# Row picks of the first two slots as two wide comparisons, with reordered first tiles, join, routing and shared slot

## The chip, the cores and the metric

One core of a Trainium2 chip runs the whole program. The metric is the device time of one execution in microseconds (us). The engines named below are PE (matrix products), DVE (vector), ACT (activation functions), POOL (GpSimd) and SP, which only issues transfers; ACT and POOL issue some transfers too.

## The reference

Three layers run one after the other: banded attention, a layer of 8 experts with 4 soft slots each, and a layer of 8 experts of which each token takes its best two.

```python
# attention: B=2, H=8, S=768, D=64; 8 global keys, 96 local ones
scores = scale * q @ k.T - slopes * dist            # masked to is_global | is_local
a = exp(scores - max); a /= a.sum + 1e-9; x = a @ v # x: [1536, 512]
# soft layer, 32 slots
logits = x @ phi
d = softmax(logits over tokens); c = softmax(logits over slots)
slot_out[e] = relu((d.T @ x)[e] @ w1[e]) @ w2[e]
x = c @ slot_out
# top-2 layer
noisy = x @ w_gate + log1p(exp(x @ w_noise)) * noise
top2 = the two largest of noisy; top2_w = softmax of the two
out[token] += top2_w * (relu(x[token] @ w1[e]) @ w2[e])   # for both experts
```

## The kernel before

Attention works on 12 tiles of 128 tokens (`NT`). The loop of `attention_near` (tile number `T`) issues by hand, for all engines: `load_k`, `load_q` and `load_v` on SP, mixed with `more_w`, which loads the first layer's weights piece by piece as `PACE` allows; `scores(T)` on PE; `maxima` (DVE) and `exps` (ACT); `inverse` (DVE, L221 and L222) and `norm` (POOL, L234); the transposes of tile T-1 (`turn`, L244, copied out at L249 or L251); the products with the values of tile T-2 (`values`, L270). A k load brings three tiles (816 KB, `KLOADS`), a v load two (512 KB, `VLOADS`); v tiles live in two buffers, so the load of tiles 4 and 5 waits until tile 2 has read tiles 0 and 1. `fill` (L398) and `warm` (L566, L799) issue matmuls whose results nobody reads; `NWARM` (L136) does so before the first tile. The bias of the scores is made from the table `dist` (L162, L165) at L392 and L402.

After the last tile `seg` and the lines from L566 join the running sums of the soft layer: a chain of small steps between PE, DVE and ACT (the join). Then `ffn_a` (L720) and `ffn_b` (L766) compute the 8 soft experts on PE in fp32; each fp32 matmul shows as two instructions, and four of them lie side by side in the array. `ffn_b` sums all experts into one PSUM tile `op` of 512 columns, which ACT (L793) and DVE (L794) copy out by halves; L803 turns the result into `soT`.

Then comes the routing, by hand on PE, DVE, ACT and POOL: noisy logits (L998 to L1013), best two (L1029, L1032), counts and positions of each token within its expert (L1035 to L1105), which give each token a `key` if it is among the rows of the first two slots (128 rows each, both of expert 0). `placed` compares the key of each of the 12 token groups with the 256 row numbers (`places`), one DVE instruction per group (L1252), into `z`; `direct` multiplies `z` with the slot weights of the tokens on PE (L1236), and L1276 copies the product out as the input of slots 0 and 1. `rows6` is a table of the row numbers, each repeated 6 times; `onehot` (L1116) uses it for the general slots. All constant tables come from `k16`, loaded at L808; ACT expands them (`table`, L1019).

From there 24 slots of 128 rows run one after the other (L1219, L1220, L1228, L1327), each with 24 products of 512 columns on PE. Beside them `rank_steps` prepares the weights of the next expert (`w_hi` on ACT L894, `w_lo` on DVE L897, `BASE` gives the place), and `Shared` (slot 24, shared by four experts, L1146 to L1202) runs within slots 18 to 21.

Of the kernel before, what the change touches and what calls it, by code (L numbers as in the profile page):

```python
# [22 lines left out]
NWARM = 16  # L23
# [5 lines left out]
KLOADS = {1: 3, 4: 6, 6: 9}  # L29
VLOADS = {0: 2, 4: 4, 6: 6, 8: 8, 10: 10}  # L30
FILL = {0: 3, 1: 4}
KP = 95
# [32 lines left out]
def emit(tc, d, near=True, stop=None):  # L65
    nc = tc.nc
    es = ExitStack()
    with es:
# [87 lines left out]
        if near:  # L156
# [5 lines left out]
            nc.sync.dma_start(out=dist[1], in_=d["dist"][1])  # L162
            load_q(1, nc.scalar)
            load_k(1)
            nc.sync.dma_start(out=dist[0], in_=d["dist"][0])  # L165
# [53 lines left out]
        def inverse(st):  # L219
            r = sm.tile([128, 4], F32, name="r", bufs=3)  # L220
            nc.vector.tensor_scalar(r, st, 1e-9, None, ALU.add)  # L221
            nc.vector.reciprocal(r, r)  # L222
            return r
# [162 lines left out]
        def attention_near():  # L386
# [24 lines left out]
            for T in range(NT + 1):  # L411
                new, b0, b1 = T < NT, 2 * T, 2 * T + 1
                more_w(PACE(b0))
                if T in KLOADS:
                    load_k(KLOADS[T], 3)
                if T + 3 < NT:
                    load_q(T + 3)
# [30 lines left out]
                for o in outs:  # L448
                    o()
                if new:  # L450
# [32 lines left out]
            fill(2, ps_t.tile([128, 512], F32, name="pt"))  # L483
            psl = logits(*SEGS[NT - 1])
            next(old)
            s_hand.close()
# [197 lines left out]
        nc.sync.dma_start(out=more, in_=d["more"])  # L684
        soT = cs2.tile([128, 4, 32], F32, name="soT")
# [52 lines left out]
        op = ps_y.tile([128, 512], F32, name="y")  # L738
# [22 lines left out]
        def ffn_b(e):  # L761
            hT = hTs.pop(e)
            for i in range(2):
                for g in range(4):
                    f = 4 * i + g
                    nc.tensor.matmul(op[32 * g:32 * g + 32, :], hT[:, f % 2, f // 2, :], units[4 * e + 2 + i][:, g],  # L766
                                     start=(e == 0 and i == 0), stop=(e == NE - 1 and i == 1), tile_position=(0, 32 * g))
# [25 lines left out]
        nc.scalar.activation(os_[:, 0:256], op[:, 0:256], AF.Copy)  # L793
        nc.vector.tensor_copy(os_[:, 256:512], op[:, 256:512])  # L794
# [13 lines left out]
        nc.sync.dma_start(out=k16, in_=d["c16"])  # L808
# [188 lines left out]

        nc.scalar.activation(ex, pl[:, :, 8:16], AF.Exp)  # L998
# [8 lines left out]
        nc.vector.scalar_tensor_tensor(t1, u_, -1.0, ex, ALU.add, ALU.subtract)  # L1007
        nc.vector.reciprocal(rc, u_)
        ttt(t1, t1, rc, ALU.mult)
        ttt(t1, t1, noise, ALU.mult)  # L1010
# [6 lines left out]
        def table(t, a):  # L1017
            n, m = t.shape[1], t.shape[2]
            nc.scalar.activation(t, k16[:, a:a + n].unsqueeze(2).to_broadcast([128, n, m]), AF.Copy)  # L1019

        table(exp24, K24)
# [11 lines left out]
        table(slot6, KSLOT)  # L1033
# [39 lines left out]
        table(rows6, 361)  # L1073
# [5 lines left out]
        K1.g_mm((2, 3))  # L1079
# [24 lines left out]
        keys = scratch([128, NT], F32)  # L1104
        ttt(keys, key16[:, 0:NT], key16[:, NT:], ALU.min)  # L1105
# [127 lines left out]
        def direct(z):  # L1233
            pct = pm_([128, 256])
            for t in range(NT):
                nc.tensor.matmul(pct, crow[:, t, 0:128], z[:, t], start=(t == 0), stop=(t == NT - 1))  # L1236
            return pct

        places = k16[:, 361:617]
# [8 lines left out]
        z = scratch([128, NT, 256], F16)  # L1248

        def placed(a, b):  # L1250
            for t in range(a, b):
                nc.vector.tensor_scalar(z[:, t], places, keys[:, t:t + 1], None, ALU.is_equal)  # L1252
# [10 lines left out]
        K1.g_scale_a()  # L1263
        placed(0, 2)
        K0.w_scale_a()
        K0.w_pow_a()
        placed(2, 4)
        K0.w_pow_b(lambda: placed(4, 5), lambda: placed(5, 6))
        placed(6, NT)
# [28 lines left out]
        def slot_y(j, hh):  # L1298
# [34 lines left out]
            if j < NOWN - 1:  # L1333
                ys = (z.rearrange("p t c -> p (t c)")[:, 1024 * j:1024 * j + 1024].bitcast(F32) if j < 2 else wk3.tile([128, 512], F32, name="ys", bufs=2) if j % 3 else
# [93 lines left out]
        def rank_steps(r):  # L1428
# [30 lines left out]
            k(6, "w_lo", 1)  # L1459
# [4 lines left out]
            k(9, "w_lo", 2)  # L1464
# [339 lines left out]
```

## Time and profile before

| what | us |
|---|---|
| median of 3 runs | 312.25 |
| lowest and highest of them | 311.44, 312.27 |
| the profiled execution | 313.0 |
| its span, first to last instruction | 310.9 |
| busy: PE, ACT, DVE, POOL | 294.2, 201.9, 199.4, 131.7 |

The profiled execution took 313.0 us, of which 310.9 are its span and 2.1 lie around it. It is 0.75 us above the median of the runs. A busy PE counts matmuls whose results nobody reads as well, so 95% says little by itself: a stage is read by what PE waited for in it, and by the transfers that landed just before. In the timeline, each line has the start, the time from start to end of a group of equal instructions, the engine, the source line, output and input; in brackets stands how long the engine sat idle before it and what released it. A letter q behind an engine's name stands for its queue, which issues transfers.

### The profile page before, as it was taken

The numbers are of one execution on the slowest core, as the hardware profiler recorded it, in microseconds if no ns is written. First come the engines' busy times: TensorE is split into PE (matmuls) and PEld (weight loads), VectorE is DVE, ScalarE is ACT, GpSimd is POOL, SyncE is SP. The second block draws the span as 40 slices with busy tenths as digits, with TensorE's granted clock in tenths as the row PEclk, the third lists the DMA queues.
The fourth block names the chain that finished last, engine by engine and source line by source line (L and its number), as shares of the span: only waits on it lengthen the run. The fifth ranks groups of instructions, "written<-read, shape, count | busy, mean of one in ns | idle before, by whom it ended". The sixth has DMA issues, their size and how long they took to land. (4 is left out here: it accounts for less than half of the span.)

```text
span 310.9 us, 7834 instructions
## 1 busy us (share of the span) xinstructions
PE 294.2 (95%) x2889; PEld 171.5 (55%) x2889; DVE 199.4 (64%) x728; ACT 201.9 (65%) x479; POOL 131.7 (42%) x169
## 2 busy tenths in 40 slices
PE   8579999999999999998999999999999999999990
PEld 3368887887765443444544445544454445544570
DVE  2868779878553000499786878879586595995110
ACT  3888977977313110499789786859688686795320
POOL 3856644754210010232726828563517335432252
PEclk9999999999998999999999999999999999999997
DMA  7999999989999999999799998498999943423444
GB/s 244 347 396 403 399 396 401 406 312 348 383 411 368 399 407 404 411 408 354 292 345 413 373 327 161 68 363 268 246 335 333 348 71 51 52 29 39 59 57 54
DMA packets 30715, 89.26 MB, mean 287 GB/s; under 512 B 2752, under 2 KB 6848, under 8 KB 30672
## 3 DMA queue, kind: packets, MB, share of 16 engines
q1 hardware_dynamic: 25840, 80.70, 67.9%
q0 software_dynamic: 4544, 7.48, 16.0%
q8 instruction: 25, 0.41, 0.5%
q10 hardware_dynamic: 288, 0.52, 0.5%
q14 instruction: 18, 0.15, 0.1%
HBM read 78.55 MB, written 10.14 MB: 285 GB/s over the span
## 5 line engine op out<-in xcount | busy, mean ns | idle before, releaser
L1327 PE MATMUL y<-w2hl,hh 128*128 128x512 f16 x528 | 119.8, 379 | 0.0
L1327 PEld LDWEIGHTS <-hh 128*128 128x128 f16 x528 | 49.8, 98 | 57.7 <-issue 3.3
L216 ACT ACTIVATE Tt<-Tt,nm 128x167 f32<-128x167 f32 x96 | 40.5, 425 | 5.2 <-DVE nm L210 5.2
L1228 DVE SCALAR_TENSOR_TENSOR hh<-h,hh 128x512 f16<-128x512 f32 x46 | 29.5, 683 | 20.6 <-ACT hh L1220 20.6
L234 POOL TENSOR_TENSOR Pb<-Tt,r 128x668 f32<-128x668 f32 x24 | 31.2, 1300 | 26.4 <-ACT Tt L216 19.2
L897 DVE SCALAR_TENSOR_TENSOR w2hl<-w,pm,w2hl 128x1024 f16<-128x1024 f32 x28 | 35.2, 1280 | 1.4 <-issue 0.7
L1345 POOL DMA_INDIRECT out_y<-ys,sidx x14 | 23.0, 1642 | 25.2 <-ACT ys L1339 17.1
L1364 POOL DMA_INDIRECT cT<-ctab,gidx x25 | 28.4, 1137 | 11.5 <-issue 5.5
L1220 ACT ACTIVATE hh<-h 128x512 f16<-128x512 f32 x46 | 25.1, 598 | 11.9 <-PE h L1219 11.9
L894 ACT ACTIVATE w2hl<-w,pm 128x1024 f16<-128x1024 f32 x28 | 31.2, 1147 | 0.2 <-DVE pm L850 0.2
L865 ACT ACTIVATE w2hl<-w 128x1024 f16<-128x1024 f32 x28 | 29.6, 1059 | 0.0
L210 DVE CUSTOM_DVE_ANT_0 Tt<-s,bias 128x167 f32<-128x167 f32 x96 | 25.7, 324 | 3.0 <-PE s L200 2.0
L1345 POOL DMA_INDIRECT out_y<-c,sidx x7 | 11.9, 1704 | 35.3 <-ACT w2hl L894 12.3
L244 PE MATMUL pt<-c,Pb 128*128 128x128 f32 x176 | 24.1, 278 | 2.6 <-ACT PT L251 1.6
L251 ACT ACTIVATE PT<-pt 128x512 f32<-128x512 f32 (+1 forms) x36 | 18.8, 556 | 9.6 <-PE pt L244 9.3
L244 PEld LDWEIGHTS pt<-c,Pb 128*128 128x128 f32 x176 | 18.8, 141 | 6.8 <-issue 3.1
L270 PE MATMUL px<-PT,vt 128*64 128x128 f32 x352 | 21.9, 276 | 0.0
L270 PEld LDWEIGHTS px<-PT,vt 128*64 128x64 f32 x352 | 19.0, 137 | 2.5 <-issue 2.0
L200 PE MATMUL s<-kx,qd 64*64 64x167 f32 x384 | 17.0, 307 | 2.6 <-DVE nm L210 1.7
L216 ACT ACTIVATION_READ_ACCUMULATOR Tt<-Tt,nm 128x1 f32 x96 | 18.2, 189 | 0.0
L756 POOL MEMSET hT<- 128x256 f32 x8 | 2.3, 311 | 35.5 <-PE y L766 23.5
L1219 PEld LDWEIGHTS <-Gst 128*128 128x128 f16 x192 | 12.7, 98 | 6.2 <-issue 0.8
(323 smaller groups left out, 482.4 us busy)
## 6 DMA issues: line engine op xcount, KB each, us to landing
w<-in_w2b SPq DMA_DIRECT2D x14, 1024.0 KB, 11.7
w<-in_w1a SPq DMA_DIRECT2D x24, 512.0 KB, 9.9
w<-in_w2a SPq DMA_DIRECT2D x12, 1024.0 KB, 10.8
x<-in_w1b SPq DMA_DIRECT2D x12, 1024.0 KB, 12.6
w<-in_w2a SPq DMA_DIRECT2D x8, 512.0 KB, 8.5
w<-in_w1a SPq DMA_DIRECT2D x4, 1024.0 KB, 10.7
vt<-in_va SPq DMA_DIRECT2D x6, 512.0 KB, 8.9
out_y<-w2hl SPq DMA_DIRECT2D x1, 3072.0 KB, 11.3
```

The lines of the kernel that those rows point to most:

```text
L210: nc.vector.tensor_tensor_reduce(S[i][:, k], bank(p, t), bias[:, int(i // 2 % 6 == 0), p, t], -0.125, 1e30, ALU.add, ALU.min, nm[:, k:k + 1])
L216: nc.scalar.activation(Tt[:, k], Tt[:, k], AF.Exp, bias=nm[:, k:k + 1], scale=-1.0, accum_out=st[:, k:k + 1])
L234: nc.gpsimd.tensor_tensor(wide(Pn, 33, 264 + 64, 528, 167), Pu.rearrange("p (a t) c -> p a t c", t=2), rb(167), ALU.mult)
L244: nc.tensor.transpose(pt[:, ch, t], Pn[:, 2 * (n % 2) + t, 136 * ch:136 * ch + 128], ident)
L270: nc.tensor.matmul(px[64 * h:64 * h + 64, p, :], vv[:, c:c + 64], cols_, start=(ch == 0 or m == 0), stop=(ch == 1))
L865: nc.scalar.activation(w2hl[:, self.r, 1, 2 * q:2 * q + 2], self.quarter(q), AF.Abs, accum_out=self.wm[:, q:q + 1])
L894: nc.scalar.activation(w2hl[:, self.r, 0, 2 * q:2 * q + 2], self.quarter(q), AF.Copy, scale=self.sw)
L897: nc.vector.scalar_tensor_tensor(w2hl[:, self.r, 1, 2 * q:2 * q + 2], self.quarter(q), self.sw, w2hl[:, self.r, 0, 2 * q:2 * q + 2], ALU.m ...
L1228: nc.vector.scalar_tensor_tensor(hh[:, 1, 4 * q:4 * q + 4], phs[q], 0.0, hh[:, 0, 4 * q:4 * q + 4], ALU.max, ALU.subtract)
L1327: nc.tensor.matmul(py, hh[:, hx, f], w2hl[:, e, wx, f], start=(n == 0), stop=(n == 23))
L1345: o = nc.gpsimd.indirect_dma_start(out=out, out_offset=bass.IndirectOffsetOnAxis(ap=sidx[:, j:j + 1], axis=0), in_=ys, in_offset=None, com ...
L1364: nc.gpsimd.indirect_dma_start(out=cgf[:, place(n)], out_offset=None, in_=ctab, in_offset=bass.IndirectOffsetOnAxis(ap=gidx[:, n:n + 1], a ...
```

## The change

The change has nine parts.

1. Start: `NWARM` goes from 16 to 9; both `dist` loads move from the SP queue to the ACT queue, in front of the second q load; the k load of tiles 3 to 5 moves from T = 1 to T = 0; each k load of the loop goes ahead of the weights of its turn; five `fill` matmuls are added in T = 1 behind the transposes.
2. `inverse`: the add of 1e-9 becomes a `scalar_tensor_tensor` with the same tile as both inputs.
3. Join: two more `fill` matmuls at the end of `attention_near`.
4. `op` becomes two tiles of 256 columns; `ffn_b` computes the first half of all columns, then the second.
5. `k16` is loaded ahead of the second layer's weights, and its three tables are expanded before the routing's first exponential, not between its steps.
6. The product with `noise` (L1010) moves from DVE to POOL and ahead of the reciprocal.
7. `placed` becomes two comparisons of 128 x 1536 elements, against `rows6`; `keys` becomes f16 with a second row, keys - 2, for the second slot; the rows of `z` are read by PE with a step of 6 elements; `direct` gets ten warming matmuls of 256 columns between its own.
8. `K1.g_mm((2, 3))` moves behind `K0.w_pow_a`, `K1.g_scale_a` behind that.
9. For the last expert `w_lo` of quarters 1 and 2 each move one place later.

```diff
-NWARM = 16
+NWARM = 9
-KLOADS = {1: 3, 4: 6, 6: 9}
+KLOADS = {0: 3, 4: 6, 6: 9}
+MORE = {1: 5}
...
             nc.sync.dma_start(out=negs, in_=d["negs"])
-            nc.sync.dma_start(out=dist[1], in_=d["dist"][1])
+            nc.scalar.dma_start(out=dist[1], in_=d["dist"][1])
+            nc.scalar.dma_start(out=dist[0], in_=d["dist"][0])
             load_q(1, nc.scalar)
             load_k(1)
-            nc.sync.dma_start(out=dist[0], in_=d["dist"][0])
...
-            nc.vector.tensor_scalar(r, st, 1e-9, None, ALU.add)
+            nc.vector.scalar_tensor_tensor(r, st, 1e-9, st, ALU.add, ALU.max)
...
-                more_w(PACE(b0))
                 if T in KLOADS:
                     load_k(KLOADS[T], 3)
+                more_w(PACE(b0))
...
                 for o in outs:
                     o()
+                fill(MORE.get(T, 0))
...
-            fill(2, ps_t.tile([128, 512], F32, name="pt"))
+            ft = ps_t.tile([128, 512], F32, name="pt")
+            fill(2, ft)
             psl = logits(*SEGS[NT - 1])
             next(old)
+            fill(2, ft)
...
         nc.sync.dma_start(out=more, in_=d["more"])
+        nc.sync.dma_start(out=k16, in_=d["c16"])
...
-        op = ps_y.tile([128, 512], F32, name="y")
+        op = [ps_y.tile([128, 512], F32, name="y")[:, 0:256] for _ in range(2)]
...
-            for i in range(2):
-                for g in range(4):
-                    f = 4 * i + g
-                    nc.tensor.matmul(op[32 * g:32 * g + 32, :], hT[:, f % 2, f // 2, :], units[4 * e + 2 + i][:, g],
-                                     start=(e == 0 and i == 0), stop=(e == NE - 1 and i == 1), tile_position=(0, 32 * g))
+            for c in range(2):
+                for i in range(2):
+                    for g in range(4):
+                        f = 4 * i + g
+                        nc.tensor.matmul(op[c][32 * g:32 * g + 32], hT[:, f % 2, f // 2, :],
+                                         units[4 * e + 2 + i][:, g, 256 * c:256 * c + 256], start=(e == 0 and i == 0),
+                                         stop=(e == NE - 1 and i == 1), tile_position=(0, 32 * g))
...
+        for t, a in ((exp24, K24), (slot6, KSLOT), (rows6, 361)):
+            n, m = t.shape[1], t.shape[2]
+            nc.scalar.activation(t, k16[:, a:a + n].unsqueeze(2).to_broadcast([128, n, m]), AF.Copy)
         nc.scalar.activation(ex, pl[:, :, 8:16], AF.Exp)
...
+        nc.gpsimd.tensor_tensor(t1, t1, noise, ALU.mult)
         nc.vector.reciprocal(rc, u_)
         ttt(t1, t1, rc, ALU.mult)
-        ttt(t1, t1, noise, ALU.mult)
...
-        keys = scratch([128, NT], F32)
-        ttt(keys, key16[:, 0:NT], key16[:, NT:], ALU.min)
+        keys = scratch([128, 2, NT], F16)
+        ttt(keys[:, 0], key16[:, 0:NT], key16[:, NT:], ALU.min)
+        nc.vector.tensor_scalar(keys[:, 1], keys[:, 0], -2.0, None, ALU.add)
...
-                nc.tensor.matmul(pct, crow[:, t, 0:128], z[:, t], start=(t == 0), stop=(t == NT - 1))
+                nc.tensor.matmul(pct, crow[:, t, 0:128], z[:, t // 6, :, :, t % 6], start=(t == 0), stop=(t == NT - 1))
+                if 0 < t < NT - 1:
+                    nc.tensor.matmul(wy[:, 0:256], warmw[:, 0:128], warmw[:, 0:256], start=True, stop=True)
...
-        z = scratch([128, NT, 256], F16)
-        def placed(a, b):
-            for t in range(a, b):
-                nc.vector.tensor_scalar(z[:, t], places, keys[:, t:t + 1], None, ALU.is_equal)
+        zf = scratch([128, 3072], F16)
+        z = zf.rearrange("p (q h r i) -> p q h r i", q=2, h=2, i=6)
+        def placed(q):
+            ttt(z[:, q], keys[:, :, 6 * q:6 * q + 6].unsqueeze(2).to_broadcast([128, 2, 128, 6]),
+                rows6.unsqueeze(1).to_broadcast([128, 2, 128, 6]), ALU.is_equal)
...
-        K1.g_scale_a()
-        placed(0, 2)
         K0.w_scale_a()
         K0.w_pow_a()
-        placed(2, 4)
-        K0.w_pow_b(lambda: placed(4, 5), lambda: placed(5, 6))
-        placed(6, NT)
+        K1.g_mm((2, 3))
+        K1.g_scale_a()
+        placed(0)
+        K0.w_pow_b()
+        placed(1)
...
-            k(6, "w_lo", 1)
+            k(6 if r < NE - 1 else 9, "w_lo", 1)
...
-            k(9, "w_lo", 2)
+            k(9 if r < NE - 1 else 10, "w_lo", 2)
```

## Rows read from the trace of the kernel before

**Rows 1.** Busy time by stretch: us, each engine's busy us (instructions), PE's granted clock, DMA share, GB/s.
```profile
20.00:40.00 20.00, 19.01 (x294) 16.31 (x296) 14.77 (x73) 16.99 (x64) 11.55 (x17) 1.00 1.03 402
...
280.00:300.00 20.00, 20.00 (x163) 10.01 (x162) 6.94 (x23) 8.58 (x12) 5.11 (x6) 1.00 0.36 48
```

**Rows 2.** Timeline of the first tiles.
```profile
1.18 4.97 PE L136 MATMUL psl<-xT 128*128 128x512 f16 x16 [1.18 <-DVE xT L133]
...
6.08 1.36 PE L200 MATMUL s<-kx,qd 64*64 64x167 f32 x32
...
6.17 0.51 DVE L392 TENSOR_TENSOR bias<-xs,negs 128x334 f32<-128x334 f32 x1 [4.63 <-DMA xs<-in_dist]
...
7.57 3.17 POOL L392 TENSOR_TENSOR bias<-xs,negs 128x668 f32<-128x668 f32 x2 [4.42 <-DMA xs<-in_dist]
...
8.05 1.53 DVE L392 TENSOR_TENSOR bias<-xs,negs 128x668 f32<-128x668 f32 x1
...
11.28 1.30 POOL L234 TENSOR_TENSOR Pb<-Tt,r 128x668 f32<-128x668 f32 x1 [0.55 <-DVE r L222]
...
11.91 0.70 DVE L221 TENSOR_SCALAR r<-st 128x4 f32<-128x4 f32 x1 [0.26 <-ACT Tt L216]
```

**Rows 3.** Timeline: the k load of tiles 3 to 5, the v load of 4 and 5.
```profile
10.11 0.72 SPq L141 DMA_DIRECT2D kx<-in_ka  x1
...
21.61 1.36 PE L200 MATMUL s<-kx,qd 64*64 64x167 f32 x32 [0.99 <-DVE PT L249]
...
30.58 0.33 SPq L153 DMA_DIRECT2D vt<-in_va  x1
...
40.96 1.97 PE L270 MATMUL px<-PT,vt 128*64 128x128 f32 x32
```

**Rows 4.** The same k load (L141) and v load (L153): us from issue to landing.
```profile
DMA to landing us min/median/max: 11.4/11.4/11.4
...
DMA to landing us min/median/max: 10.5/10.5/10.5
```

**Rows 5.** Timeline of the join: three warming matmuls on PE.
```profile
88.49 0.81 PE L566 MATMUL pt<-c 128*128 128x512 f16 x3
```

**Rows 6.** Busy time behind the join by stretch of 1 us (columns as in rows 1).
```profile
93.00:94.00 1.00, 1.00 (x16) 0.56 (x12) 0.41 (x2) 0.52 (x1) 0.00 (x0) 0.50 1.02 406
...
96.00:97.00 1.00, 1.00 (x24) 0.64 (x20) 0.00 (x0) 0.00 (x0) 0.00 (x0) 0.95 1.01 410
```

**Rows 7.** Timeline of the soft experts and of the copies of their sum.
```profile
109.67 3.66 PE L720 MATMUL h<-w,siT 128*32 128x256 f32 x64
...
118.01 7.07 PE L766 MATMUL y<-w,hT 128*32 128x512 f32 x64
...
125.20 0.38 ACT L793 ACTIVATE w<-y 128x256 f32<-128x256 f32 x1 [11.27 <-DMA k<-in_c]
...
125.62 0.42 DVE L794 COPY w<-y 128x256 f32<-128x256 f32 x1 [7.14 <-ACT w L793]
```

**Rows 8.** Timeline of the routing.
```profile
130.61 0.26 DVE L1010 TENSOR_TENSOR w2hl<-w2hl,more 128x96 f32<-128x96 f32 x1
...
138.57 0.73 DVE L1252 TENSOR_SCALAR w2hl<-k,w2hl 128x256 f16<-128x256 f16 x2
...
140.90 1.57 DVE L1252 TENSOR_SCALAR w2hl<-k,w2hl 128x256 f16<-128x256 f16 x6
...
142.82 0.42 DVE L1276 CAST w2hl<-m 128x256 f16<-128x256 f32 x1 [0.36 <-PE m L1236]
```

**Rows 9.** Lines L1116 and L1288: duration in ns, min/median/max, first and last start.
```profile
L1116 DVE TENSOR_TENSOR w2hl<-w2hl,rows x4: 553/554/558, 144.1 to 146.5; 128x768 f16<-128x768 f16 x4
...
L1288 PEld LDWEIGHTS <-w2hl x24: 124/126/147, 145.6 to 147.5; 128*128 128x128 f16 x24
```

**Rows 10.** Timeline around the shared slot's first product.
```profile
271.78 1.27 DVE L1228 SCALAR_TENSOR_TENSOR hh<-h,hh 128x512 f16<-128x512 f32 x2
...
272.51 0.55 PE L1172 MATMUL h<-ct,x 128*128 128x32 f16 x16 [0.41 <-DVE hh L1228]
```

More of the change, by code (lines that the diff above doesn't have):

```diff
@@ L792, in emit @@
         os_ = wb.tile([128, 2048], F32, name=f"w{NWA + NW}")
-        nc.scalar.activation(os_[:, 0:256], op[:, 0:256], AF.Copy)
-        nc.vector.tensor_copy(os_[:, 256:512], op[:, 256:512])
+        nc.scalar.activation(os_[:, 0:256], op[0], AF.Copy)
+        nc.vector.tensor_copy(os_[:, 256:512], op[1])
         wy = ps_y.tile([128, 512], F32, name="y")
@@ L807, in emit @@
             nc.gpsimd.dma_start(out=d["o_so"], in_=soT.rearrange("p a s -> p (a s)"))
-        nc.sync.dma_start(out=k16, in_=d["c16"])
         raw0.update({i: load_part(0, i, ring((i + 2) % 4)) for i in (2, 3)})
@@ L1015, in emit @@
         nc.scalar.activation(gs0[:, 0:1], ex[:, 0, 0:1], AF.Exp)
[L1017 to L1021, printed above, removed]
         K0.w_abs(0)
@@ L1032, in emit @@
             nc.vector.max_index(out=i8[:, t], in_max=m8[:, t], in_values=nl[:, t])
-        table(slot6, KSLOT)
         id24 = cs2.tile([128, 2, NT], F16, name="id24")
@@ L1072, in emit @@
         K0.w_abs(3)
-        table(rows6, 361)
         nc.gpsimd.tensor_scalar(gts[:, 0], e2, 1.0, 1e-9, ALU.add, ALU.add)
@@ L1078, in emit @@
             K0.g_mid(i, pst[i])
-        K1.g_mm((2, 3))
         for i in range(2):
@@ L1235, in direct @@
             for t in range(NT):
-                nc.tensor.matmul(pct, crow[:, t, 0:128], z[:, t], start=(t == 0), stop=(t == NT - 1))
+                nc.tensor.matmul(pct, crow[:, t, 0:128], z[:, t // 6, :, :, t % 6], start=(t == 0), stop=(t == NT - 1))
+                if 0 < t < NT - 1:
+                    nc.tensor.matmul(wy[:, 0:256], warmw[:, 0:128], warmw[:, 0:256], start=True, stop=True)
             return pct
-        places = k16[:, 361:617]
         def gates_a():
@@ L1333, in slot_y @@
             if j < NOWN - 1:
-                ys = (z.rearrange("p t c -> p (t c)")[:, 1024 * j:1024 * j + 1024].bitcast(F32) if j < 2 else wk3.tile([128, 512], F32, name="ys", bufs=2) if j % 3 else
+                ys = (zf[:, 1024 * j:1024 * j + 1024].bitcast(F32) if j < 2 else wk3.tile([128, 512], F32, name="ys", bufs=2) if j % 3 else
                       cs2.tile([128, 512], F32, name="c16"))
```

## The prediction

> **What bounds the kernel now.** I read the busy time by stretch first, because it says which stages can give anything back. From slot 2 to the end PE is never idle: the stretch from 280 to 300 shows 20.00 of 20 us [rows 1]. So a change ahead of the slots is worth what it brings forward the first slot's input, no more, and a change inside the slots only what PE waits for there. The stretch from 20 to 40 shows two things side by side: PE 19.01 of 20, and the DMA share 1.03 at 402 GB/s [rows 1]. In the attention both are full, so there I read next which loads land just in time. Between the soft experts and the slots PE waits for chains of small steps; there the timeline gives each step and its releaser.
>
> **Part 1, start and k load.** The first scores start at 6.08, when the 16 warm-ups, which run from 1.18 to 6.15, are through; DVE waits 4.63 us for `dist`, until 6.17 [rows 2]. With 9 warm-ups and `dist` on a queue of its own both can start a little earlier; I put that at 0.2 to 0.5 us (the first k tile needs its landing too). The larger step is tile 3. Its k load is issued at 10.11 and takes 11.4 us to land, so it lands at 21.51; PE, which sat idle for 0.99 us, starts tile 3 at 21.61 [rows 3, 4]. The profile names a DVE copy as releaser, but the landing fits better. Issued one tile earlier, and ahead of the weights, this load is no longer late. So PE could reach tile 3 about 1.0 + 0.2 = 1.2 us earlier.
>
> What is late next? The v load of tiles 4 and 5 is issued at 30.58 and lands 10.5 us later, at 41.08; the products of tile 6's turn, whose second half needs it, start at 40.96 [rows 3, 4]. That load has no slack. Its bytes stand behind the same bytes as before: the change only orders loads among those in front of it, and the DMA is full in this stretch [rows 1]. If PE comes 1.2 us earlier, it waits there. So the bounds for the whole attention are 0.0 and -1.2 us. I take -0.5: nearer to the landing of the v load, with something left for the stream starting a little sooner. The five added matmuls lie where PE waits for the exponentials of tile 1; at about 0.21 us each (three take 0.81 [rows 5]) they are 1.1 us, which that wait hides. Uncovered they would cost that, and end in the same wait at the v load.
>
> **Part 2, inverse.** One of its 24 adds took 0.70 us instead of 0.16, starting at 11.91 while POOL's 1.30 us product from 11.28 ran [rows 2]: the two cannot run at once. The new form reads two tiles from SBUF. The trace has that case too: the 668-element DVE product at 8.05 took 1.53 us beside POOL's two, where the 334-element one took 0.51 alone, so at most 1.02 was its own and about 0.5 was waiting [rows 2]. So the new form waits as the old one did: 0.0, and -0.5 at best, in tile 1, which the v load takes back. The Trainium skill says the same against this edit, in "SBUF — State Buffer", section "Who interferes with whom": a vector instruction with two SBUF inputs contends with a GpSimd instruction that reads SBUF. The trace agrees (1.53 us); without that rule the edit would be worth 0.5 us at tile 1.
>
> **Part 3, join.** Two more warm-ups are 2 x 0.21 = 0.4 us of PE [rows 5]. If they stand in front of the chain's next product, they delay it by that; if they fall into a wait, they are free. Bounds 0.0 and +0.4; I take +0.2. What they may buy is the clock: in 93 to 94, the first of three such rows up to 96, PE ran at 0.50, which is the lower level of 1.2 GHz, with 16 instructions per us; in 96 to 97 it ran at 0.95, nearly the 2.4 GHz level, with 24 [rows 6]. Before it fell PE had done a run of tiny products. Three us at half speed cost 1.5 us. I don't count on it: the added matmuls come several us ahead of the fall, and what lies between stays as thin as it was. It is a rival.
>
> **Part 4, two halves of the sum.** Before, the last product ends at 118.01 + 7.07 = 125.08, ACT copies from 125.20 to 125.58, and DVE, waiting for ACT, from 125.62 to 126.04 [rows 7]. After, the first half is complete about 0.9 us before the end (a quarter of the last expert pair's products), ACT's copy hides behind the rest, and DVE's starts 0.12 behind PE's end. Gain: 126.04 - 125.08 - 0.12 - 0.42 = 0.4. Cost: 64 instructions of 512 columns take 7.07, 64 of 256 columns 3.66 [rows 7]; two halves against a whole are 0.25 us more for 64, mostly the last one's way through, which a block pays once. For all 128 that is 0 to +0.5; I take +0.1. Part 4 is -0.3, between +0.1 and -0.4.
>
> **Part 5, tables.** ACT expands them in the wait before the routing, in the shadow of PE, if `k16` has landed; it is issued several us earlier than before. On the chain of the routing DVE was the one waited for, so what ACT saves there gives 0.0. If `k16` came late, ACT's first exponential would come late by as much.
>
> **Part 6, noise on POOL.** One DVE step of 0.26 us leaves the chain, with its issue 0.29 [rows 8]; POOL's product lies beside the reciprocal. I take -0.3; the worst is 0.0, if POOL's result comes as late as DVE's would.
>
> **Part 7, picks.** Before, twelve picks run from 138.57 to 140.90 + 1.57 = 142.47 and the copy of their product starts 0.35 later, at 142.82 [rows 8]. The last six take 0.26 each; twelve are 3.1, and the 0.8 left are the steps of the weights' scale and waits for POOL (the first two took 0.73). After, two comparisons of 1536 elements: the same form with 768 takes 0.554 [rows 9], so two of double size cost at most 2 x 1.11 and, since part of 0.554 is fixed, about 2 x 0.95. With 0.1 for the second row of keys, 0.8 for the other steps and 0.1 more for POOL, they end at 138.57 + 0.1 + 1.9 + 0.8 + 0.1 = 141.5, 1.0 us earlier. But then PE has more to do: before, one product was left; now six and the five warming ones between them. At half of 0.21 us each, ten more are 1.1. So the copy starts at 141.5 + 0.35 + 1.1 = 142.95: +0.1 us, later than before. Most of what DVE saves PE spends. Unknown is the read at a step of 12 bytes. The nearest row is the weight load of L1288 with the same step: 126 ns for 128 columns [rows 9], which for 256 is 0.25 instead of 0.11. The bounds are then -0.1 and +0.1 + 6 x 0.14 = +0.95. I take +0.2. The Trainium skill's "SBUF — State Buffer", section "Door 1: The DMA port swizzle", says that accesses need two hits on a 16-byte line to run at full rate, and a step of 12 bytes mostly gives one; it states no size, and no run here shows one for the moving operand.
>
> **Part 8** moves 1.07 us of PE work between the two comparisons, where PE waits anyway: 0.0; if the comparisons were quick enough to catch it, up to +0.3. **Part 9:** PE waits 0.41 us at 272.1 for DVE's step that starts at 271.78 [rows 10], because a `w_lo` of 1.27 us runs ahead of it. Moved behind, it frees DVE; the last expert's weights are needed two slots later. -0.4, at worst 0.0.
>
> **Sum.** -0.5 + 0.2 - 0.3 - 0.3 + 0.2 - 0.4 = -1.1 us. Against the profiled execution of 313.0 (span 310.9 and 2.1 around it) that is 311.9. The median of the runs is 0.75 lower, so I forecast 312.25 - 1.1 = 311.15. About 0.3%, 0.94 us, can be told from no change here.
>
> **Rivals.** (a) The v load isn't the limit: the attention gives all its 1.2, 0.7 more, 310.45. For it: landing and use differ by 0.1 us, and a median hides how the bytes are ordered. Against it: the full DMA. (b) The join keeps PE at 2.4 GHz: 1.5 more, 309.65. For it: only a few matmuls were missing. Against it: they come early. (c) Slower: the step of 12 bytes makes each product of the picks several times as long. From 0.45 us per product (0.34 more, times six, 2.05) the whole turns slower by over 0.3%; at 0.5 us it is 311.15 + 6 x 0.39 = 313.5. For it: at this step hardly two columns lie close together. Against it: the 126 ns of the nearest row. The section of the Trainium skill's "SBUF — State Buffer" named in part 7 points the same way. (d) The comparisons don't run at the rate of L1116, or the read costs the 0.95: 0.75 to 1.5 us more, 311.9 to 312.65, no change. Against it: the operands have the form of L1116.
>
> **Numbers.** The forecast has 0.45, with its own range of 310.5 to 311.8; (a) 0.18, (b) 0.15, (c) 0.08, (d) 0.10, and 0.04 stay for a mishap that I don't see. Faster by over 0.3% is below 311.3: 0.26 of the forecast, (a) and (b), 0.59. Slower is (c) and the rest, 0.12; within it 0.29. The range reaches from 309.4, which takes in (b), to 312.7, which takes in (d).
>
> **What would show it.** Right: PE starts tile 3 about 1 us earlier and waits at the products of tile 6's turn for the v load; DVE's copy of the sum starts without ACT; the copy of the picks' product starts over 1 us behind the end of the second comparison; no wait at the shared slot's second product. Wrong: tile 6 comes as much earlier as tile 3 (a); the granted clock stays at 1.00 behind the join (b); products of the picks over 0.4 us apart (c); a comparison of over 1.2 us (d).

## The result

The changed kernel takes 314.69 us (median; 312.70 to 319.83) where the kernel before, run beside it, took 312.22. Four of its 20 executions were over 1.5% slower than its fastest and, as in every ratio below, such slow ones are left out: the ratio is 1.0057 with a 95% interval of 1.0032 to 1.0082, about 1.8 us slower. The forecast was 1.1 us faster. Its profiled execution took 314.76 us, 312.9 of them its span.

The profile after, first the join, the copies of the experts' sum and the routing's first steps (timeline: start, us, engine, line, output and input; in brackets the idle time before and its releaser). Lines lie a few numbers later than before: the copies of [rows 7] are L800 and L801, the picks of [rows 8] L1255, their copy L1280.

```profile
86.46 0.28 PE L588 MATMUL px<-rmb,c 128*128 128x4 f32 x2
...
114.84 7.11 PE L772 MATMUL y<-w,hT 128*32 128x256 f32 x128
...
121.20 0.38 ACT L800 ACTIVATE w<-y 128x256 f32<-128x256 f32 x1 [10.46 <-PE y L772]
...
122.02 0.42 DVE L801 COPY w<-y 128x256 f32<-128x256 f32 x1 [6.72 <-PE y L772]
...
125.34 0.25 ACT L1007 ACTIVATE w2hl<-m 128x96 f32<-128x96 f32 x1 [2.56 <-PE m L995]
```

DVE's copy starts 3.60 us earlier than in [rows 7]. Of that, 1.35 us are the earlier join and 0.47 the split sum; the rest is mostly the granted clock, which behind the join stood at 0.50 for some 3.4 us in the profile before [rows 6], a loss of 1.7 us, and stayed at 1.00 in this one. Then the picks, DVE first and PE below:

```profile
134.63 0.17 DVE L1106 TENSOR_TENSOR w2hl<-w2hl 128x12 f16<-128x12 f16 x1
134.83 0.49 DVE L1107 TENSOR_SCALAR w2hl<-w2hl 128x12 f16<-128x12 f16 x1
...
135.46 1.12 DVE L1255 TENSOR_TENSOR w2hl<-w2hl,rows 128x1536 f16<-128x1536 f16 x1
...
137.22 0.95 DVE L1255 TENSOR_TENSOR w2hl<-w2hl,rows 128x1536 f16<-128x1536 f16 x1
...
142.12 0.42 DVE L1280 CAST w2hl<-m 128x256 f16<-128x256 f32 x1 [3.94 <-PE m L1238]
```
```profile
136.76 0.84 PE L1238 MATMUL m<-w2hl,c 128*128 128x256 f16 x2
137.42 0.29 PE L1240 MATMUL y<-c 128*128 128x256 f16 x1
137.55 0.50 PE L1238 MATMUL m<-w2hl,c 128*128 128x256 f16 x1
137.87 0.29 PE L1240 MATMUL y<-c 128*128 128x256 f16 x1
138.00 0.50 PE L1238 MATMUL m<-w2hl,c 128*128 128x256 f16 x1
```

The second comparison ends at 138.17, 4.30 us earlier than the last pick before (142.47, [rows 8]). But PE is then still at its fourth product of twelve: with a warming product between, they come 0.45 us apart, and DVE sits 3.94 us idle for them. The copy starts at 142.12, only 0.70 us earlier than in [rows 8], and that is owed to the clock: in the third profile of the changed kernel, where it fell behind the join as it did before, the copy starts at 143.72, 0.90 us later than in [rows 8]. From keys to copy the change takes 7.5 us.

The 0.70 us do not reach the end either. At 162.17 PE waits 0.79 us for the input of slot 3 (counted from 0; the expectations below call it the third slot), where it did not wait before. The last POOL instruction ends 0.26 us later than before, and the span ends 6.3 us behind it; in other profiled executions, of this kernel and of others below, that tail is 4.5 to 6.3 us, with no order by kernel that I can see.

### The profile page after: what moved, and what is told of

It is laid out like the page before. It is cut to its first block, busy times and chain, and to the rows that moved or that the text cites. A ratio compares the mean times of both kernels' runs of the same rounds, so it can differ in the third digit from the quotient of the medians.

```text
span 312.9 us, 8102 instructions
## 1 busy us (share of the span) xinstructions
PE 296.8 (95%) x3027; PEld 176.5 (56%) x3027; DVE 198.5 (63%) x718; ACT 202.2 (65%) x479; POOL 133.1 (43%) x170
## 5 line engine op out<-in xcount | busy, mean ns | idle before, releaser
L1368 POOL DMA_INDIRECT cT<-ctab,gidx x25 | 27.3, 1093 | 12.2 <-DVE pm L850 5.9
L1349 POOL DMA_INDIRECT out_y<-c,sidx x7 | 12.8, 1834 | 33.9 <-DVE hh L1230 8.0
```

The source lines that it names most:

```text
L1349: o = nc.gpsimd.indirect_dma_start(out=out, out_offset=bass.IndirectOffsetOnAxis(ap=sidx[:, j:j + 1], axis=0), in_=ys, in_offset=None, com ...
L1368: nc.gpsimd.indirect_dma_start(out=cgf[:, place(n)], out_offset=None, in_=ctab, in_offset=bass.IndirectOffsetOnAxis(ap=gidx[:, n:n + 1], a ...
```

## The experiments

Every ratio is to the kernel before, run beside it on the same chip; intervals are 95%. Four chips took part: one for the first three experiments and the changed kernel's second profile; one for the steps, the attention part alone and the two runs on the fill; one for the picks alone, the first run of the paired picks, the old attention and the low weights; one for the four runs that share a chip. Times from different chips are not set side by side, only ratios.

### The picks put back: the change without its loss

```diff
-            ttt(z[:, q], keys..., rows6..., ALU.is_equal)
+            for t in range(6 * q, 6 * q + 6):
+                nc.vector.tensor_scalar(z[:, t], places, keys[:, t:t + 1], None, ALU.is_equal)
...
-                nc.tensor.matmul(pct, crow[:, t, 0:128], z[:, t // 6, :, :, t % 6], ...)
-                if 0 < t < NT - 1:
-                    nc.tensor.matmul(wy[:, 0:256], warmw[:, 0:128], warmw[:, 0:256], start=True, stop=True)
+                nc.tensor.matmul(pct, crow[:, t, 0:128], z[:, t], ...)
```

> The changed kernel with its picks alone put back: one key per block of tokens, twelve comparisons that write each block's 256 columns side by side, twelve products over neighbouring columns, no warming products between them; all else as changed. In the trace of the changed kernel the keys are written at 134.63 us and the first product's result is copied at 142.12 us, 7.5 us later; in the kernel before the same way took 138.32 to 142.82 us, 4.5 us. Theory A (the picks' strided products are what the change lost): the way from keys to copy is again about 4.5 us, the copy comes near 139.2 us, 2.9 us earlier than in the changed kernel, and the time falls by 2 to 3 us, to 311.7 to 312.7 us, or below the kernel before. Rival B (what is lost lies behind the picks, where the changed kernel lost its lead of 0.7 us between 154 and 162 us and 1.7 us behind the last instruction): the copy comes earlier all the same but PE waits for it again in the first slots, and the time stays within 0.7 us of 314.7 us.

Measured: 309.77 us, 0.9924 (0.9893 to 0.9955). Timeline of its picks:

```profile
135.71 0.17 DVE L1106 TENSOR_TENSOR w2hl<-w2hl 128x12 f32<-128x12 f16 x1
...
136.11 1.53 DVE L1255 TENSOR_SCALAR w2hl<-k,w2hl 128x256 f16<-128x256 f16 x6
...
138.22 1.56 DVE L1255 TENSOR_SCALAR w2hl<-k,w2hl 128x256 f16<-128x256 f16 x6
140.14 0.42 DVE L1279 CAST w2hl<-m 128x256 f16<-128x256 f32 x1 [0.36 <-PE m L1237]
```

Twelve single comparisons take 3.09 us where the two wide ones took 2.07; yet keys to copy is 4.43 us, not 7.49. Theory A holds: between keys and copy the new picks lose 3.06 us. The ratios lie further apart, 0.0133 or some 4 us; the runs on one chip below come back to that. The kernel without its new picks beats both. Layout, comparisons, strided read and warming products are all put back here; the next three experiments separate them.

### Wide comparisons, columns side by side

```diff
-            ttt(z[:, q], keys[:, :, 6 * q:6 * q + 6].unsqueeze(2).to_broadcast([128, 2, 128, 6]), rows6..., ALU.is_equal)
+            ttt(z[:, 6 * q:6 * q + 6], keys[:, 6 * q:6 * q + 6].unsqueeze(2).to_broadcast([128, 6, 256]),
+                mid_bc(places, 6), ALU.is_equal)
...
-                nc.tensor.matmul(pct, crow[:, t, 0:128], z[:, t // 6, :, :, t % 6], ...)
-                if 0 < t < NT - 1:
-                    nc.tensor.matmul(wy[:, 0:256], warmw[:, 0:128], warmw[:, 0:256], start=True, stop=True)
+                nc.tensor.matmul(pct, crow[:, t, 0:128], z[:, t], ...)
```

> The changed kernel with two wide comparisons that write each block's 256 columns side by side (the key repeated along the columns, the row numbers repeated over the six blocks), twelve products over neighbouring columns, no second key and no warming products. Theory A (the read in steps of 12 bytes makes a product dear): products are 0.11 us apart as in the kernel before, where twelve went by in two groups of 1.35 and 1.25 us; the copy comes 2.5 to 3.5 us earlier than in the changed kernel and the time is 311.5 to 313 us. The comparison itself may cost more: 0.95 us in the changed kernel where both operands run along the columns, up to 1.6 us where the key stands still. Rival C (the wide comparisons and what waits for them, not the read, make the picks late): the copy comes within 0.7 us of 142.1 us and the time stays at 314 to 315.5 us.

Measured: 311.02 us, 0.9991 (0.9958 to 1.0024). The first two lines are DVE's comparisons, the other two PE's products:

```profile
134.87 1.90 DVE L1254 TENSOR_TENSOR w2hl<-w2hl,k 128x1536 f16<-128x1536 f16 x1
137.33 1.75 DVE L1254 TENSOR_TENSOR w2hl<-w2hl,k 128x1536 f16<-128x1536 f16 x1
...
136.83 0.84 PE L1237 MATMUL m<-w2hl,c 128*128 128x256 f16 x6 [0.59 <-DVE w2hl L1254]
139.13 0.83 PE L1237 MATMUL m<-w2hl,c 128*128 128x256 f16 x6 [1.46 <-DVE w2hl L1254]
```

Six products take 0.84 us, so the read and the warming products were the cost; rival C falls. But with the key standing still along the columns a comparison takes 1.75 to 1.90 us, above the 1.6 I had set as its upper end, and PE now waits for DVE: the copy starts at 139.99, 2.1 us earlier than in the changed kernel and not theory A's 2.5 to 3.5.

### The strided products without the warming ones

```diff
-                if 0 < t < NT - 1:
-                    nc.tensor.matmul(wy[:, 0:256], warmw[:, 0:128], warmw[:, 0:256], start=True, stop=True)
```

> The changed kernel without the ten warming products between the twelve strided ones. In its trace a strided product and a warming one take 0.45 us together, and a warming one 0.13 us to the next. Theory A (the strided read is the cost): products 0.30 to 0.32 us apart, the twelve in 3.8 us in place of 5.3, the copy 1.3 to 1.5 us earlier, the time 0.5 to 1.5 us lower. Rival D (the switch between two kinds of products is the cost): products fall to 0.11 to 0.15 us, the copy comes 3.5 us earlier, the time is 2 to 3 us lower.

Measured: 312.00 us, 1.0017 (0.9987 to 1.0047). The twelve products, and then busy time by stretch (columns as in rows 1):

```profile
136.71 4.24 PE L1238 MATMUL m<-w2hl,c 128*128 128x256 f16 x12
```
```profile
141.00:142.00 1.00, 0.54 (x11) 0.53 (x10) 0.97 (x7) 0.11 (x1) 0.39 (x1) 1.00 0.33 135
142.00:143.00 1.00, 0.76 (x8) 0.31 (x6) 1.00 (x5) 1.00 (x3) 0.00 (x0) 0.79 0.74 286
143.00:144.00 1.00, 1.00 (x4) 0.39 (x3) 0.97 (x4) 1.00 (x2) 0.00 (x0) 0.50 1.13 247
```

Products come 0.34 us apart: theory A, not D. The copy starts at 140.99, and the ratio is 0.0040 below the changed kernel's, some 1.2 us, as theory A had it. But in this execution the granted clock then fell to 0.50, the 1.2 GHz level, after PE had done nothing but strided products for 4.2 us and then waited for the copy; slot 3 started at 161.25, no earlier than in the second profile of the changed kernel (copy at 142.17, slot 3 at 161.21). So in this execution the 1.2 us that the ten warming products cost were lost to the clock instead. That the strided products brought it down is not shown: in the run with columns side by side it fell at the same place, and there no product was strided and PE had waited 2.05 us for DVE (same columns):

```profile
142.00:143.00 1.00, 1.00 (x4) 0.40 (x3) 0.97 (x4) 1.00 (x2) 0.00 (x0) 0.50 1.03 331
```

### The price of a step

The edit is to the kernel with the old picks; one execution was profiled.

```diff
-                nc.tensor.matmul(pct, crow[:, t, 0:128], z[:, t], ...)
+                w = (1, 2, 3, 4, 6, 8)[t // 2]
+                nc.tensor.matmul(pct, crow[:, t, 0:128], zf[:, 0:256 * w].rearrange("p (c i) -> p c i", i=w)[:, :, 0], ...)
```

> The kernel with the old picks, but its twelve products read the 256 columns with steps of 1, 2, 3, 4, 6 and 8 elements of f16 (2 to 16 bytes), two products each; what they give for the first two slots is therefore not what is wanted, and only the time of a product is read here. Without warming products between them the strided ones of the experiment before took 4.24 us for twelve, 0.33 to 0.35 each, the contiguous ones 0.11. Theory A1 (the cost grows with the bytes spanned by the read): 0.11, 0.11 to 0.12, 0.17, 0.23, 0.34, 0.45 us for the six steps. Theory A2 (one price as soon as neighbouring elements do not lie side by side): 0.11 for step 1 and about 0.33 for all others.

The pairs of products in order of step, 2, 4, 6, 8, 12 and 16 bytes (start of the first, time to the modelled end of the second):

```profile
136.57 0.39 PE L1238 MATMUL m<-w2hl,c 128*128 128x256 f16 x2
...
136.79 0.39 PE L1238 MATMUL m<-w2hl,c 128*128 128x256 f16 x2
...
137.02 0.50 PE L1238 MATMUL m<-w2hl,c 128*128 128x256 f16 x2
...
137.36 0.62 PE L1238 MATMUL m<-w2hl,c 128*128 128x256 f16 x2
...
137.80 0.86 PE L1238 MATMUL m<-w2hl,c 128*128 128x256 f16 x2
...
138.48 1.08 PE L1238 MATMUL m<-w2hl,c 128*128 128x256 f16 x2
```

From one pair's start to the next, halved: 0.11, 0.115, 0.17, 0.22 and 0.34 us for 2, 4, 6, 8 and 12 bytes. The last pair has no successor; its 1.08 us, from which the first pair's way through of 0.17 (0.39 less 2 x 0.11) is taken off, give some 0.45 by an estimate. Theory A1: up to 4 bytes a step costs nothing, beyond that the time grows with the bytes spanned, three times as much at 12. The Trainium skill, "SBUF — State Buffer", section "Door 1: The DMA port swizzle", says that two accesses to one 16-byte line are enough for the full rate, and gives 8 bf16 as how far one can stride for free; the run, in f16, does not agree, since at 8 bytes, two elements to a 16-byte line, a product already takes twice as long. Weighed against this kernel, the page's rule gave the right sign for 12 bytes and no size.

### A step that is free

```diff
+        rows2 = scratch([128, 256, 2], F16)
...
+            ttt(z[:, 3 * q:3 * q + 3],
+                keys[:, 6 * q:6 * q + 6].rearrange("p (t i) -> p t i", i=2).unsqueeze(2).to_broadcast([128, 3, 256, 2]),
+                rows2.unsqueeze(1).to_broadcast([128, 3, 256, 2]), ALU.is_equal)
...
+                nc.tensor.matmul(pct, crow[:, t, 0:128], z[:, t // 2, :, t % 2], ...)
```

> The picks of the changed kernel done with a step that costs nothing: two wide comparisons with a table of all 256 places repeated twice, blocks laid in pairs, so that a product reads with a step of 4 bytes, which took 0.11 us in the experiment on steps; no second key, no warming products. Theory A (the read's step alone made the wide comparisons a loss): comparisons near 1 us each, where six single ones take 1.53 to 1.56 us, products 0.11 us apart, keys to copy 3.4 to 4 us where the old picks took 4.4 us; the time 0 to 0.9 us below the kernel with the old picks (309.77 us, 0.992 of the kernel before). Rival I (a comparison over pairs loses the speed that it has over rows of six, as it did with a key standing still, 1.75 to 1.90 us): keys to copy 4.8 to 5.5 us, the time 0.3 to 1 us above the old picks.

Measured: 312.20 us, 0.9985 (0.9955 to 1.0015), on a chip where the kernel before took 313.44. Its keys, first comparison, first six products and copy:

```profile
135.23 0.17 DVE L1107 TENSOR_TENSOR w2hl<-w2hl 128x12 f16<-128x12 f16 x1
...
135.60 1.13 DVE L1255 TENSOR_TENSOR w2hl<-w2hl 128x1536 f16<-128x1536 f16 x1
...
136.91 0.87 PE L1238 MATMUL m<-w2hl,c 128*128 128x256 f16 x6
...
139.19 0.42 DVE L1281 CAST w2hl<-m 128x256 f16<-128x256 f32 x1 [0.95 <-PE m L1238]
```

Comparisons of 1.13 and 0.95 us, six products in 0.87, keys to copy 3.96 us: as theory A had it in the trace. By its ratio it was slower than theory A's 0.992 or less, but the old picks had run on another chip. So both ran once more on one chip:

> The paired wide picks on the same chip as the old picks. Keys to copy took 3.96 us in their profile against 4.43 with the old picks. Theory O (the copy still sets the end): 0.3 to 0.6 us faster than the old picks. Rival P (from there on the third slot's gather sets the end, so that an earlier copy is given back as a wait for the third slot): within 0.3 us of the old picks, with a wait of 0.5 to 1 us ahead of the third slot's first product.

> The changed kernel with the old picks, on the same chip. Theory A with parts that add up: 0.992 to 0.996 of the kernel before. Rival N (the 0.992 was a lucky sample and the parts without the picks are worth nothing): 0.998 to 1.001.

Paired 311.34 us, 0.9939 (0.9904 to 0.9973); old picks 311.02 us, 0.9938 (0.9908 to 0.9968). The same; 0.9938 is theory A's, not rival N's. Counted from the join, the paired picks are ahead by 0.50 us at the first slot's first product (52.59 against 53.09 us), and still by 0.48 at slot 3's (73.32 against 73.80) and at the end of the last POOL instruction. Both profiles wait 0.92 us for slot 3's input (PE; the old picks, then the paired ones):

```profile
160.04 0.61 PE L1220 MATMUL h<-ct,Gst 128*128 128x128 f16 x8 [0.92 <-DVE ct L1128]
```
```profile
159.91 0.61 PE L1221 MATMUL h<-ct,Gst 128*128 128x128 f16 x8 [0.92 <-DVE ct L1129]
```

So the wait that rival P named is there, but it is as long with the old picks, and the lead is not given back in it: these two traces speak for theory O. Their executions took the same time all the same (310.82 and 310.87 us), because the join of the paired one came 0.34 us later. In the medians 0.3 us either way is within what these runs tell, so it is not settled.

### Picks alone, and the changed kernel on one chip with the others

> The kernel before with the pick part alone (second key, two wide comparisons over the row table, strided products with ten warming products, tables and their constants' load moved ahead of the exponential as this needs). In the kernel before keys to copy took 4.5 us (138.32 to 142.82), in the changed kernel 7.5 us (134.63 to 142.12). Theory A (strided products are the loss): the way from keys to copy is about 7.5 us again, and the time rises by 2 to 3.2 us over the kernel before. Rival B (the loss comes from the earlier join, that is from the picks meeting other work in another order): keys to copy 4.5 to 6 us, the time 0 to 1.5 us above the kernel before.

Measured: 1.0142 (1.0091 to 1.0193), about 4.4 us slower, from fewer executions than the others (6). Keys 138.12, copy 145.62: 7.50 us, as in the changed kernel. From keys to copy the part costs the same with the early join and without it; rival B falls. The time lies above theory A's 2 to 3.2 us, of which the interval takes in the upper end (2.9).

> The changed kernel once more, for a second profiled execution. If the 1.7 us by which one piece of the last store landed late (span 312.9 us, last instruction of GpSimd ended at 306.6 us) and the 0.8 us wait for the third slot at 161.4 us belong to the kernel, both are there again; if they belong to the one execution, they are gone and the span is near 311 us.

Measured: 313.12 us, span 311.3. Copy at 142.17, no wait for slot 3 (161.21), tail 5.7 us. The 7.5 us of the picks belong to the kernel. The wait for slot 3 comes in some of its executions only: it was gone here, and in the third profile, of the run below, it is back with 0.86 us, at a tail of 5.3.

> The changed kernel on one chip with the three below. It took 1.0057 of the kernel before. Theory A (3 us lost from keys to copy, less 1.2 us or more won in the attention part): 1.004 to 1.008, and 3 to 4 us more than with the old picks.

Measured: 315.30 us, 1.0062 (1.0029 to 1.0096). As theory A had it. Against the old picks beside it that is 0.0124 of 313.2, 3.9 us for the pick part, 0.8 more than the 3.06 of the traces. The clock can be what is missing: in 7 of the 12 executions of the changed kernel its mean over the execution lay below 0.990, and in none of the 12 with the old picks. The means of the two groups are 0.9901 and 0.9939; 0.0038 of 313 us are 1.2 us, by an estimate. In which stage it fell in them no trace tells.

### The attention and the rest

> The kernel before with the attention part alone (nine warming products ahead, five later, the three keys a tile earlier, distances on ScalarE's queue, keys ahead of weights, the fused guard of the inverse). The prediction gave this part 0.5 us, with a full gain of 1.2 us if no load of values holds it up; profiles of the changed kernel put the join 0.3 to 1.5 us earlier than in the kernel before. Theory E (the earlier tiles carry to the join): 0.8 to 1.4 us faster than the kernel before. Rival F (the load of values for tiles 4 and 5 and the granted clock at the join take it back): 0 to 0.5 us faster.

Measured: 309.93 us, 0.9961 (0.9929 to 0.9992), and on the last chip:

> The attention part alone, on the same chip; it gave 0.996 before. If the rest of the change without the picks is worth nothing (0 us), it equals the kernel with the old picks within 0.002; if the rest is worth its forecast of 0.5 to 1 us, it lies 0.0015 to 0.003 above it.

Measured: 0.9956 (0.9925 to 0.9988), 1.4 us. Theory E. On that chip the kernel with the old picks lies 0.0018, 0.6 us, below it: what the rest may be worth, inside the intervals. The profiles of these two show the rest up to the copy: from the join to the copy of the picks' product 53.36 us with the attention part alone and 52.61 with the rest, 0.75 us less, at a granted clock of 1.00 in both.

> The kernel with the old picks and the attention part put back as in the kernel before; what is left of the change is the fill at the end of the attention, the split of the experts' sum in two banks, the tables, the noise product on GpSimd, the order of routing and the last expert's low weights. With the attention part it took 0.992 of the kernel before, and the attention part alone gave 0.996. Theory L (the parts add up): 0.995 to 0.998, 0.6 to 1.5 us below the kernel before. Rival M (only the attention part is worth anything, the rest of the difference is scatter): 0.999 to 1.001.

Measured: 1.0015 (0.9979 to 1.0052), nearest to rival M, with theory L's 0.998 just inside the interval. So by the times most of the gain there is lies in the attention part; a rest of some 0.6 us is not excluded.

### The fill at the join

```diff
-            fill(2, ps_t.tile([128, 512], F32, name="pt"))
+            ft = ps_t.tile([128, 512], F32, name="pt")
+            fill(2, ft)
             psl = logits(*SEGS[NT - 1])
             next(old)
+            fill(2, ft)
```

> The kernel before with two more filling products at the end of the attention alone. In its profile PE ran at half the granted clock for 3.4 us after the join; half of that, 1.7 us, is lost where PE sets the time. Theory G (the fill keeps the clock up at the join): the mean granted clock of most executions rises from 0.988 to 0.994 or more, and the time falls by 0.6 to 1.6 us. Rival H (the fill costs its 0.3 to 0.4 us and the clock falls as often as before): 0 to 0.4 us slower, clocks as before.

> The kernel with the old picks without the two filling products at the end of the attention. It took 309.77 us with them, 0.992 of the kernel before, and no execution had a mean granted clock under 0.990. Theory G (the fill keeps the clock up): clocks of 0.988 come back in most executions and the time rises by 0.5 to 1.5 us. Rival H: clocks stay at 0.990 and above and the time falls by 0 to 0.4 us.

Measured: with the fill alone 1.0004 (0.9979 to 1.0029); the old picks without it 0.9942 (0.9910 to 0.9973), with it 0.9924 and 0.9938 on other chips. No difference in either time. Of the clocks, 8 of 12 executions with the fill alone had a mean of 0.994 or more, and 13 of 29 of the kernel before beside them, too few to tell; without the fill 1 of 12 fell below 0.990, where theory G had most. The changed kernel's first profile kept the clock behind the join, its third did not (busy time by stretch, columns as in rows 1; first and third profile):

```profile
93.00:94.00 1.00, 1.00 (x24) 0.65 (x20) 0.91 (x3) 0.08 (x1) 0.00 (x0) 1.00 1.01 397
```
```profile
92.00:93.00 1.00, 1.00 (x12) 0.43 (x8) 0.62 (x2) 0.31 (x1) 0.00 (x0) 0.50 0.81 324
```

With the fill in both, the clock falls in some executions and not in others; some 3 us at half the clock, as in [rows 6], cost 1.5 us. The times fit rival H; theory G's 0.6 to 1.6 us are not there.

### The last expert's low weights

```diff
-            k(6 if r < NE - 1 else 9, "w_lo", 1)
+            k(6, "w_lo", 1)
...
-            k(9 if r < NE - 1 else 10, "w_lo", 2)
+            k(9, "w_lo", 2)
```

> The kernel with the old picks and the low weights of the last expert back in their old place. The prediction gave their move 0.4 us, the wait of PE at 272.51 us in the kernel before. In the traces with the move that wait is gone, but the copies of shared weights on DVE come 0.25 us later and PE's products with them (277.8 and 280.8 us) start 0.3 us late and run slower. Theory J (DVE sets this stretch, so that the wait only moves): the wait of 0.4 us is back, the late products are gone, the time stays within 0.2 us of the old picks' 309.8 us. Rival K (the move gains what was forecast): the time rises by 0.4 us.

Measured: 0.9964 (0.9927 to 1.0001) on a chip where the old picks had not run, so by time it is open. The traces show it. With the move, in the changed kernel, the wait of [rows 10] is gone (first line), and the copies of shared weights and their products come late (DVE, then PE):

```profile
271.80 0.95 PE L1174 MATMUL h<-ct,x 128*128 128x32 f16 x32
```
```profile
280.36 1.42 DVE L1184 COPY w<-w2hl 128x1024 f16 x4
...
280.83 0.73 PE L1192 MATMUL pg<-w,x 128*32 128x512 f16 x3
```

Put back, the same products are on time and the wait is there again:

```profile
270.83 0.55 PE L1173 MATMUL h<-ct,x 128*128 128x32 f16 x16 [0.41 <-DVE hh L1229]
...
279.18 0.44 PE L1191 MATMUL pg<-w,x 128*32 128x512 f16 x3
```

DVE works without a pause from 272 to 281 us in either; the 1.27 us that were moved behind one step stand ahead of another. From the shared slot's first product to the third block of the next ones PE takes 11.95 us with the move (271.80 to 283.75) and 11.95 without it (269.87 to 281.82): theory J, by the trace.

## Why the prediction was wrong

**The step that failed** is part 7's price of the read, and with it the count. I bounded a product at a step of 12 bytes by the nearest row, the weight load at that step [rows 9], as at most 0.25 us. It is 0.34. A weight load there took 126 ns, where the picks' contiguous ones took 97 (median, old picks), a third more; the operand that streams through takes three times as long. The row was near by its step and far by its operand. And I counted six products behind the second comparison. That holds only if the first six fit beside it: at 0.45 us with the warming ones between them they end long after it (the fifth starts at 138.44, when DVE is done), so that all twelve and the ten stand in the way, 5.4 us from the first to the copy. From the end of the second comparison to the copy I had 1.45 us; it took 3.95. Forecast for keys to copy: 4.7 us (138.32 to 143.0); measured 7.5. The comparisons themselves were right (0.95 and 1.12 us for the forecast 0.95 to 1.11); they ended 3.5 us behind the keys for the forecast 3.2, since the second row of keys alone took 0.49 for the forecast 0.1.

This is rival (c), "products of the picks over 0.4 us apart", with the sign and the mechanism it named, and a chance of 0.08. Not with its price: the 0.45 us have a warming product in them, and a strided product by itself takes 0.34, 0.23 more than a contiguous one where (c) began at 0.34 more. Its 2.05 us were too low all the same, by the count: against the old picks the trace gives 3.06. The rows did not exclude a threefold price, so it should have had more.

**Part 1** gave more than forecast, and not where I had read it. The runs gave 1.2 to 1.4 us, rival (a)'s size; in the profile tile 3 starts 1.80 us earlier than in [rows 3] and the join 1.35. But the wait of 0.99 us ahead of tile 3, from which I took 1.0 us, stands in the one profile that I read. The kernel with the fill alone has the attention of the kernel before, with the k load at T = 1, and there tile 3 starts 5.14 us behind tile 2, as in the changed kernel (starts of tiles 2 and 3, fill alone, then after):

```profile
16.59 1.37 PE L200 MATMUL s<-kx,qd 64*64 64x167 f32 x32
...
21.73 1.36 PE L200 MATMUL s<-kx,qd 64*64 64x167 f32 x32
```
```profile
14.67 1.37 PE L201 MATMUL s<-kx,qd 64*64 64x167 f32 x32
...
19.81 1.37 PE L201 MATMUL s<-kx,qd 64*64 64x167 f32 x32
```

The picks alone and the old attention show the same 5.1 us. So that the k load set tile 3 is true of one profile of four. Tile 2 is 1.25 us earlier already, in the mean of the fourteen profiles with the part against the four without, and the join 1.07 (86.53 against 87.60). By these traces the part gains in tiles 0 to 2; which of its edits does it, no run separates. The 1.35 us compare two profiles: the first line shown under the result, at 86.46, and this one of the kernel before:

```profile
87.81 0.35 PE L584 MATMUL px<-rmb,c 128*128 128x4 f32 x2
```

What I also missed is that the v load is not fixed. It is issued when tile 2 has read its buffers, so it moved with the tiles:

```profile
29.67 0.33 SPq L154 DMA_DIRECT2D vt<-in_va  x1
...
39.16 2.14 PE L271 MATMUL px<-PT,vt 128*64 128x128 f32 x32
```

Issued 0.91 us earlier than in [rows 3], it held tile 6's products up by only 0.17 us here (2.14 for 1.97). In the profile of the old picks PE waited 0.79 us for it at 40.64, and in six of the fourteen profiles with the part 0.16 to 0.82; in the four without it never. So the bound that I forecast is there, but later and smaller than I put it.

**Part 2** was right: the new add took 0.69 us at 11.18 where the old took 0.70 [rows 2]. **Part 3**, +0.2, lies within the measured nothing. Rival (b)'s sign, a clock of 1.00 behind the join, stood in the first profile and was gone in the third; its 1.5 us are in none of the runs on the fill. **Part 4**: from the last product's end to the end of DVE's copy 0.96 us before [rows 7], 0.49 after, 0.47 gained for the forecast 0.4; the 128 products took 7.11 us for 7.07. **Part 6**: from the exponential to the best two 2.89 us before, 2.67 after, 0.2 for the forecast 0.3. Together these 0.7 us agree with the 0.75 of the two traces from the join to the copy and with the 0.6 of the runs, but the runs cannot tell that from nothing. **Part 5** was right: the tables run from 121.48 to 122.78, before the exponential at 125.34. **Part 8**, 0.0, fits the trace: the picks' first product starts 0.18 us behind the end of the first comparison (136.76, 136.58), so the moved work did not hold it up. **Part 9** was wrong: the wait went, and came back 8 us later at the next step that DVE serves. I named what was moved, but not what then stood behind it on DVE.

The sum with the measured terms: -1.4 for the attention, +3.9 for the picks, -0.6 for the rest, 1.9 us slower; the same chip gave 1.0062, 1.9 us. The three are differences of runs on that chip, so the sum is no proof. By the traces it is 3.06 for the picks, less 0.75 for the rest and 1.07 to 1.35 for the join: 1.0 to 1.2 us slower. The 0.7 to 0.9 us that are left over are not shown in any trace; the clock's estimated 1.2 us would cover them.

## What to carry to other kernels

Before a layout is changed to suit the engine that writes it, price the engine that reads it: here DVE won 1 us and PE lost 4. A price for an access pattern counts only from a row of the same operand of the same kind of instruction; where there is none, give the case "as many times slower as the bytes it spans" a real chance. And when a step gets dearer, count again how many of its instructions still hide behind the work beside them. A wait is priced only when a second profile of the kernel has it too: the one ahead of tile 3 was gone in three of four.

## What the runs showed of the hardware

A product of 256 columns of f16 took 0.11 us at steps of 2 and 4 bytes, 0.17 at 6, 0.22 at 8 and 0.34 at 12, while a weight load of 128 columns took 126 ns at 12 bytes [rows 9] against 97 contiguous. A comparison of 1536 elements of f16 took 0.95 to 1.18 us with the key repeated outside pairs or sixes and 1.75 to 1.90 with it repeated along the innermost columns. After 4.2 us of strided products alone, in which PE counted as busy throughout, and a wait for the copy, the granted clock fell from 2.4 to 1.2 GHz in the profiled execution; with the ten contiguous products between them it stayed up there in all three profiles. It fell at the same place with contiguous products and 2.05 us of waits ahead of it, so what brings it down is open. Behind the join it fell in some profiles of the same kernel and not in others.
